# Block-sorted attention and a gated MLP: a new order of units, with whole K copies, an earlier range check and one batch's q turned by DMA

## The chip, the cores and the metric

The kernel runs on one core of a Trainium2 chip. The metric is the device time of one launch in microseconds, as the median of several runs. A core has five engines, each with its own queue of instructions that it works through in order: TensorE (PE, the matrix products; its weight loads are shown as PEld), VectorE (DVE), ScalarE (ACT), GpSimd (POOL) and SyncE (SP). Sixteen DMA engines move data between the memories. In this kernel POOL issues the loads from the chip's main memory and SP issues all other transfers.

## The reference

Each batch of attention first makes an 8x8 mixing matrix P per head by five rounds of exponential, row and column scaling. P mixes the eight blocks of k and of v. Attention runs inside each of the eight blocks. Its output is the input of a gated MLP, whose second half is normalised by row, mixed along the sequence by w_spatial, and multiplied with the first half before the last product.

```python
# attention per batch b and head h (B=4, H=8, S=768, D=64, 8 blocks of 96 rows)
P = sort_net
for _ in range(5):
    P = P - np.max(P, axis=-1, keepdims=True)
    P = np.exp(P)
    P = P / (np.sum(P, axis=-1, keepdims=True) + 1e-09)
    P = P / (np.sum(P, axis=-2, keepdims=True) + 1e-09)
...
k_sorted = np.einsum('bhij,bhjcd->bhicd', P, k_b).reshape(B, H, S, D)
v_sorted = np.einsum('bhij,bhjcd->bhicd', P, v_b).reshape(B, H, S, D)
...
scores = scale * np.matmul(q_b, k_sb.transpose(0, 1, 2, 4, 3))
scores = scores - np.max(scores, axis=-1, keepdims=True)
attn = np.exp(scores)
attn = attn / (np.sum(attn, axis=-1, keepdims=True) + 1e-09)
return np.matmul(attn, v_sb).reshape(B, H, S, D).astype(np.float32)
...
# gated MLP on x = the attention's output as (B, S, 512)
h = np.maximum(x @ w_in, 0.0)                     # w_in 512 x 1024
u, v = (h[..., :d_ff // 2].copy(), h[..., d_ff // 2:].copy())
mu = np.mean(v, axis=-1, keepdims=True)
var = np.mean((v - mu) ** 2, axis=-1, keepdims=True)
v_n = (v - mu) / np.sqrt(var + 1e-06)
v_s = np.einsum('ts,bsd->btd', w_spatial, v_n) + b_spatial[None, :, None]
gated = u * v_s
return (gated @ w_out).astype(np.float32)         # w_out 512 x 512
```

## The kernel before

The kernel is a list of short units, written as one string, ORDER (lines 18 to 48). A loop at line 692 reads it from left to right and calls the function u_NAME with the arguments behind the colons. Each unit appends its instructions to the queues of the engines that it uses, so the string fixes the order of work on every engine, on SP and on POOL's loads too; engines wait for one another through semaphores that the framework sets by tiles. Nothing is reordered afterwards.

The units, with their lines, are these. The number just behind the name is mostly one of four PSUM tiles ps0 to ps3 (two banks each); a letter is the engine of a copy (A is ACT, D is DVE, P is POOL); b is the batch, 0 to 3, and hp one of four pairs of heads.

- S0 loads sort_net. CO, ID, MA, MB, MC and IV fill constants. SK:n (L223) is round n of the scaling, alternating ACT and DVE.
- L (L156) issues a load on POOL: q, k and v of a batch (a tile of 768 KB in bf16 from a pool of eight, "ld"), both halves of w_in (wv for the normalised half, wu for the other), both halves of w_spatial (wsa, wsb), and w_out (wo).
- DM (L216) is a run of products on zeros, which nobody reads.
- PR and P0, PC, PD (L246 to L279) spread P into the matrices pd, by batch. P0 is on DVE for batch 0, PC copies P to SBUF, PD builds the later batches' pd on POOL from that copy. There are two pd tiles.
- QT and QQ (L311, L317) turn q on PE: 12 transposes for each pair of heads, then a copy out of PSUM. QT does one pair, QQ two.
- QP and QX (L337, L348) are another way to turn q, and the old order doesn't use them: QP copies a pair of heads on POOL or DVE into an ld tile in another order, and QX turns the pairs in one transposing DMA issued by SP.
- KT and VT (L370, L373) are 12 products that mix and turn k or v, with a copy by natural (L292). Its letters name the engines of the copy: with two letters, as in KT:2:DA:0:1, the first engine copies the first half of the columns and the second the rest.
- VM and VC: VM (L386) is v mixed in its natural layout, VC (L400) moves it by SP into vb, the operand of attention, one transfer for each of the blocks named.
- SC (L414) is the scores of a pair of heads and four blocks, and the exponential on ACT. AT (L459) is the product with v, the reciprocal of the sums and the scaling on DVE.
- XT and XD (L491, L482) turn the attention's output, on PE or by a transposing DMA.
- WT (L501) turns w_spatial. VP (L507) is x times the v half of w_in, for one or two row tiles of 128; ST, LN and LA (L525 to L547) are its statistics and normalisation. UP (L549) is the u half.
- SP (L564) is the mixing by w_spatial and the addition of the bias (BI loads it) into z on DVE. GT (L581) is u times z on DVE or POOL.
- OP (L588) is the last product, in some places cut into terms 0 to 3 and 3 to 4. OE (L602) copies it out of PSUM, in halves at the end, into one of two o tiles, and OS (L608) stores it by SP.
- CK (L617) tests that the attention's sums and the scaling's first sums lie in a safe range: ten small DVE instructions. CF (L632) adds up the findings with a product and leaves an integer flag. LF (L638) reads this flag into a register of every engine. At line 696 every engine branches on it: where the flag isn't zero, general_path computes everything again in a slower and safer way. BH (L641) marks a branch hint on PE and DVE.

The K copy that the change touches, and the flag read:

```python
for n, e in enumerate(eng):
    x = slice(n * 128 // len(eng), (n + 1) * 128 // len(eng))
    copy(e, to[:, x], of[:, x])
...
st["beyond"] = nc.values_load(flag[0:1, 0:1], min_val=0, max_val=512)
...
with tc.If(st["beyond"] > 0, preferred_fallthrough_block=True, label="general"):
    general_path()
```

Of the kernel before, what the change touches and what calls it, by code (L numbers as in the profile page):

```python
# [15 lines left out]


ORDER = """
S0 CO SK:0 L:q:0:0:8 L:k:0:0:8 L:v:0:0:8 L:v:1:0:8 BH SK:1 SK:2 L:k:1:0:8 ID IV:2 MC IV:0 DM:1:6:512 L:q:1:0:8 SK:3
L:wv MA DM:3:6:512 DM:1:6:512 DM:2:6:512 SK:4 L:wsb QT:1:A:0:0 MB QT:0:D:0:1 QT:3:A:0:2 DM:2:6:512 PR:3 DM:2:6:512  # L20
P0:0:2 KT:1:A:0:0 P0:6:8 L:wu P0:4:6 PC:D P0:2:4 PD:1:0:4 QT:0:D:0:3 L:wsa IV:1 PD:1:4:8 KT:2:DA:0:1 KT:3:DA:0:3
SC:1:0:0:0 SC:0:0:1:1 KT:2:D:0:2 SC:3:0:0:1 L:q:2:0:8 VT:1:D:0:0 SC:0:0:2:0 L:k:2:0:8 VT:2:D:0:1 SC:3:0:3:1 VB:1:D:0:0
VT:0:A:0:2 VB:2:D:0:1 VT:3:A:0:3 AT:1:0:0:1 VB:0:A:0:2 L:v:2:0:8 AT:2:0:0:0 L:wo VB:3:D:0:3 PD:3:0:4 SC:1:0:3:0
AT:0:0:1:1 SC:2:0:1:0 SC:3:0:2:1 AT:1:0:3:1 VM:2:A:1:0 AT:0:0:1:0 VM:3:A:1:1 AT:1:0:2:1 VM:2:A:1:2 XT:0:D:0:1:0
KT:3:A:1:2 AT:1:0:2:0 KT:0:A:1:0 AT:2:0:3:0 XT:3:A:0:1:2 KT:0:A:1:3 QQ:1:D:1:0 VM:2:A:1:3 XT:0:D:0:0:2 XT:3:D:0:0:0
SC:1:1:0:0 QQ:2:D:1:2 VC:1:0:4 KT:0:A:1:1 VP:1:D:0:0:1 SC:3:1:2:1 ST:0:0 SC:0:1:3:1 VP:2:A:0:4:5 WT:3:A:5 WT:1:D:4
VP:0:A:0:3 ST:0:5 PD:2:0:4 SC:2:1:1:0 ST:0:3 SC:1:1:2:0 UP:3:A:0:1:0 VP:2:A:0:2 VC:1:4:8 ST:0:1 ST:0:4 AT:0:1:0:0
ST:0:2 WT:1:A:3 SC:3:1:3:0 LN:0:0:6 UP:2:A:0:0:1 AT:0:1:2:0 AT:1:1:3:0 LA:0:0 PD:2:4:8 UP:3:A:0:1:1 WT:0:D:0 LA:0:2
LA:0:1 LA:0:4 AT:2:1:2:1 LA:0:3 XT:1:A:1:0:2 LA:0:5 L:v:3:0:8 WT:3:A:1 UP:0:A:0:0:0 WT:3:D:2 BI SC:1:1:0:1 QQ:2:A:2:2
AT:3:1:1:0 AT:0:1:3:1 SP:1:0:3 SC:2:1:1:1 XT:0:D:1:1:2 XT:3:A:1:0:0 AT:1:1:0:1 AT:2:1:1:1 SP:0:0:2 XT:2:A:1:1:0  # L30
GT:P:0:3 KT:1:AD:2:3 KT:3:AD:2:2 KT:0:DA:2:0 KT:2:A:2:1 GT:P:0:2 QQ:1:A:2:0 SC:0:2:3:0 VM:3:D:2:3 SP:2:0:1 VM:1:A:2:2
VM:0:A:2:1 VP:3:D:1:0:1 VM:2:A:2:0 SP:1:0:0 SC:0:2:2:1 SC:2:2:1:1 GT:P:0:1 VC:2:4:8 VC:2:0:4 ST:1:1 VP:3:A:1:4:5
SC:1:2:1:0 SC:0:2:3:1 GT:P:0:0 UP:2:A:1:0:0 PD:3:4:8 ST:1:0 ST:1:4 VP:3:D:1:2:3 VM:2:A:3:3 VM:1:A:3:0 OP:0:0:2 ST:1:2
OE:A:0:2 L:k:3:0:8 AT:1:2:3:1 VM:2:A:3:2 UP:3:A:1:1:0 ST:1:5 AT:0:2:2:1 ST:1:3 VM:2:D:3:1 L:q:3:0:8 UP:1:A:1:0:1
AT:3:2:1:1 LN:1:0:6 UP:0:A:1:1:1 LA:1:1 AT:1:2:3:0 OP:2:0:0 LA:1:0 SC:1:2:0:1 SC:0:2:2:0 OP:3:0:4 LA:1:5 OS:0:2
OE:D:0:0 LA:1:3 LA:1:4 LA:1:2 AT:2:2:0:1 AT:0:2:2:0 SP:1:1:0 OE:A:0:4 XD:2:1 SC:2:2:0:0 KT:0:DA:3:2 QQ:3:D:3:2
KT:1:D:3:1 KT:2:AD:3:0 SP:0:1:2 KT:2:A:3:3 OS:0:4 GT:D:1:0 QQ:1:A:3:0 AT:3:2:1:0 AT:0:2:0:0 VP:2:D:2:4:5 VC:3:0:4
VC:3:4:8 SC:3:3:3:0 SC:1:3:3:1 ST:2:4 XD:2:0 SP:0:1:1 SC:2:3:2:1 GT:D:1:2 SC:1:3:1:1 SP:3:1:3 AT:0:3:3:0 GT:P:1:3
AT:2:3:3:1 VP:1:A:2:2:3 ST:2:5 VP:0:A:2:0:1 OS:0:0 AT:1:3:2:1 GT:P:1:1 ST:2:3 UP:2:D:2:0:1 OP:1:1:2 SC:3:3:0:0
OE:D:1:2 ST:2:2 SC:2:3:1:0 UP:0:A:2:1:0 SC:1:3:0:1 ST:2:1 ST:2:0 LN:2:0:6 SC:3:3:2:0 UP:2:D:2:0:0 AT:0:3:1:1 LA:2:5  # L40
LA:2:4 LA:2:2 OS:1:2 UP:1:A:2:1:1 OP:2:1:0 AT:1:3:0:0 OE:A:1:0 LA:2:0 LA:2:3 LA:2:1 OP:3:1:4 AT:2:3:1:0 AT:0:3:2:0
SP:1:2:1 XD:3:0 AT:2:3:0:1 XD:3:1 GT:D:2:1 OE:A:1:4 SP:0:2:0 SP:1:2:3 GT:D:2:0 SP:0:2:2 OS:1:4 UP:3:D:3:0:0 OS:1:0
VP:0:D:3:2:3 GT:D:2:2 VP:1:A:3:0:1 ST:3:3 GT:D:2:3 ST:3:2 UP:3:A:3:0:1 VP:0:A:3:4:5 ST:3:1 OP:3:2:2 ST:3:0 OP:2:2:0
ST:3:5 ST:3:4 OE:A:2:2 LN:3:0:6 UP:1:A:3:1:1 LA:3:1 UP:0:A:3:1:0 LA:3:5 LA:3:3 LA:3:0 LA:3:2 OE:A:2:0 LA:3:4 SP:1:3:2
SP:3:3:0 GT:P:3:2 SP:0:3:1 OP:2:2:4 GT:D:3:1 OS:2:0 OS:2:2 OE:A:2:4 GT:D:3:0 SP:3:3:3 OP:1:3:0:0:3 GT:D:3:3
OP:0:3:4:0:3 OP:-1:3:0:3:4 OE:A:3:0:1:2 OP:3:3:2:0:3 CK OS:2:4 OP:-1:3:2:3:4 OE:D:3:2:1:2 OE:A:3:0:0:1 OP:-1:3:4:3:4
OS:3:0:1:2 OS:3:0:0:1 OE:A:3:2:0:1 OS:3:2:0:1 OS:3:2:1:2 OE:A:3:4:0:1 OS:3:4:0:1 OE:A:3:4:1:2 OS:3:4:1:2 CF:2 LF
"""


# [677 lines left out]
```

## Time and profile before

| what | value |
|---|---|
| median of 3 runs | 164.26 us (164.16 to 164.29) |
| the profiled execution | 163.99 us, its span 162.2 us |
| DVE, ACT, POOL busy | 117.7, 84.3, 33.7 us |
| TensorE's granted clock, mean | 0.988 |
| read from main memory, written to it | 24.78 MB, 6.29 MB |
| q copies on ACT and DVE (two pairs, L107 and L109) | 1447 and 957 ns each |
| K copies, whole, on ACT and DVE | 800 and 952 ns each |
| K copies, half, on ACT and DVE | 482 and 549 ns each |
| gate product on POOL and on DVE (L585) | 1640 and 948 ns each |
| transposing DMA (L486), issue to landing | 4.6 to 5.5 us |

The span runs from the first to the last instruction in the trace, and the profiled time is a little longer than it. Times in a trace are counted from the start of the span. The chain that ended last is found by going back from the last instruction to whatever released it, again and again, so a stretch of PE in it means that PE was the engine that everything waited for. The busy time of an engine that is not on the chain can fill up or empty without any effect on the time.

### The profile page before, as it was taken

How to read it: one execution, taken by the hardware profiler on the slowest of the kernel's cores; microseconds unless marked ns; L12 is line 12 of the kernel's file. 1: busy time of each engine (PE TensorE's matmuls, PEld its weight loads, DVE VectorE, ACT ScalarE, POOL GpSimd, SP SyncE). 2: the span in 40 equal slices, each digit the busy share in tenths (PEclk: the TensorE clock that was granted, in tenths of full speed). 3: DMA queues.
4: the chain of work that ended last, by engine and by line, in shares of the span. 5: the costliest groups of instructions: out<-in, count | busy, mean ns of one | idle time of the engine just before them, and what ended most of it. 6: DMA issues, size and time to landing. Idle time of an engine off the chain costs nothing.

```text
span 162.2 us, 3967 instructions
## 1 busy us (share of the span) xinstructions
PE 147.9 (91%) x1646; PEld 89.5 (55%) x1657; DVE 117.7 (73%) x265; ACT 84.3 (52%) x118; POOL 33.7 (21%) x39
## 2 busy tenths in 40 slices
...
DMA  2999999999999990479985996002059200243370
GB/s 12 191 204 205 203 205 205 210 220 237 271 206 204 206 172 0 69 133 148 184 188 94 225 149 195 0 36 97 0 107 237 113 0 0 91 172 129 129 250 25
DMA packets 27351, 23.20 MB, mean 143 GB/s; under 512 B 7232, under 2 KB 24128, under 8 KB 27328
## 3 DMA queue, kind: packets, MB, share of 16 engines
...
q14 instruction: 9, 0.07, 0.1%
HBM read 24.78 MB, written 6.29 MB: 192 GB/s over the span
## 4 chain that ended last, share of the span: by engine, by line
PE 78%; ACT 7%; DVE 6%; DMA 2%; issue 2%; DVEq 0%; ACTq 0%
PE ps L569 20%; PE ps L557 13%; PE ps L514 13%; PE ps L595 11%; PE ps L468 4%; PE ps L422 4%; PE ps L363 3%; PE ps L390 3%; PE ps L307 3%; ACT ex L427 2%; ACT kt L107 2%; PE ps L498 2%; DMA out_dram<-o_sb 1%; PE ps L504 1%; ACT o_sb L107 1%
## 5 line engine op out<-in xcount | busy, mean ns | idle before, releaser
L569 PE MATMUL ps<-wspT,v_sb 128*128 128x384 bf16 x192 | 33.2, 326 | 0.0
L427 ACT ACTIVATE ex<-ps 96x768 bf16<-96x768 f32 x32 | 24.4, 806 | 12.4 <-PE ps L422 12.3
L585 POOL TENSOR_TENSOR gt<-z,u_sb 128x768 bf16<-128x768 f32 x7 | 11.4, 1640 | 92.7 <-DVE z L575 42.1
L569 PEld LDWEIGHTS <-v_sb 128*128 128x128 bf16 x192 | 18.2, 98 | 11.9 <-issue 0.2
L575 DVE TENSOR_TENSOR z<-ps,b_bc 128x768 f32<-128x768 f32 x16 | 15.3, 957 | 11.6 <-PE ps L569 11.5
L557 PE MATMUL ps<-xT,w_in_sb 128*128 128x384 bf16 x128 | 23.3, 326 | 0.0
L476 DVE TENSOR_TENSOR x_sb<-ps,rec_all 96x512 bf16<-96x512 f32 x32 | 22.0, 687 | 1.1
L514 PE MATMUL ps<-w_in_sb,xT 128*128 128x512 bf16 x89 | 22.2, 379 | 0.4
L595 PE MATMUL ps<-w_out_sb,gt 128*128 128x512 bf16 x93 | 22.0, 379 | 0.2
L107 ACT COPY o_sb<-ps 128x1024 f32<-128x1024 f32 (+1 forms) x12 | 9.8, 835 | 14.8 <-PE ps L595 12.9
L531 DVE BATCH_NORM_STATS2 stats<-v_sb 128x6 f32<-128x512 bf16 x24 | 16.2, 677 | 1.0 <-ACT v_sb L113 0.9
L113 ACT ACTIVATE v_sb<-ps 128x1024 bf16<-128x1024 f32 (+1 forms) x8 | 7.4, 920 | 17.6 <-PE ps L514 17.6
L557 PEld LDWEIGHTS <-w_in_sb 128*128 128x128 bf16 x128 | 11.8, 98 | 7.6
L595 PEld LDWEIGHTS <-gt 128*128 128x128 bf16 x96 | 9.2, 98 | 10.2
L514 PEld LDWEIGHTS <-xT 128*128 128x128 bf16 x96 | 9.0, 98 | 9.6 <-DVE x_sb L476 0.2
L113 ACT ACTIVATE u_sb<-ps 128x768 bf16<-128x768 f32 x13 | 10.6, 812 | 5.1 <-PE ps L557 5.0
L107 ACT CAST kt<-ps 128x768 bf16<-128x768 f32 (+1 forms) x14 | 8.7, 641 | 7.9 <-PE ps L363 5.5
L468 PEld LDWEIGHTS <-ex 96*128 96x128 bf16 x256 | 10.5, 97 | 3.6 <-issue 0.3
L468 PE MATMUL ps<-vb,ex 96*128 96x65 bf16 x256 | 11.9, 193 | 0.1
L219 PE MATMUL ps<-warm 128*128 128x512 bf16 x35 | 9.9, 436 | 1.3 <-DVE warm L192 1.3
L422 PE MATMUL ps<-qT,kt 64*128 64x96 bf16 x256 | 9.5, 204 | 1.6 <-ACT kt L107 1.3
L422 PEld LDWEIGHTS <-kt 64*128 64x128 bf16 x256 | 6.2, 94 | 6.9 <-issue 3.8
...
## 6 DMA issues: line engine op xcount, KB each, us to landing
...
```

Of the source, the lines that this page charges most:

```text
L107: nc.scalar.copy(out=out, in_=in_)
L113: nc.scalar.activation(out=out, in_=in_, func=AF.Relu)
L422: nc.tensor.matmul(t[:, hh, 0:HW].rearrange("p (g x) -> p g x", g=G)[:, :, ii * TB:(ii + 1) * TB], lhsT=kT[rows, i * BLK:i * BLK + 128], r ...
L427: nc.scalar.activation(out=e_tile(b, hp, ih).rearrange("p h (x g) -> p h x g", g=G), in_=t[0:BLK, :, 0:HW].rearrange("p h (g x) -> p h x g ...
L468: nc.tensor.matmul(t[:, hh, ii * VW:ii * VW + D + 1], lhsT=e[:, c:c + 128], rhs=vb[b % 2][:, ih * NI + ii, 2 * hp + hh, 0:D + 1], start=Tr ...
L476: nc.vector.tensor_mul(out=x_sb[:, hp].rearrange("p i (h d) -> p h i d", h=2), in0=tv[:, :, :, 0:D], in1=_raw_ap(rec, 0, [rec.ap[0], [NI, ...
L514: nc.tensor.matmul(t[:, x, :], lhsT=st["xT", b][:, n // 3, kc, (n % 3) * 128:(n % 3 + 1) * 128], rhs=w_in_sb[:, kc, DH:DFF], start=(kc == ...
L531: nc.vector.bn_stats(out=stats, in_=st["v_sb", b, n])
L557: nc.tensor.matmul(t[:, x, 0:HW], lhsT=w_in_sb[:, kc, mc * 128:(mc + 1) * 128], rhs=st["xT", b][:, ih, kc, :], start=(kc == 0), stop=(kc = ...
L569: nc.tensor.matmul(t[:, x, 0:HW], lhsT=st["v_sb", b, n][:, mc * 128:(mc + 1) * 128], rhs=wspT[:, 3 * x:3 * x + 3, n, :], start=(n == 0), s ...
L575: nc.vector.tensor_add(out=z.rearrange("p (x c) -> p x c", x=2), in0=t[:, :, 0:HW], in1=b_bc.rearrange("p (x c) -> p x c", x=2),)
L595: nc.tensor.matmul(t[:, x, :], lhsT=st["gt", b, mc][:, (n0 + x) * 128:(n0 + x + 1) * 128], rhs=w_out_sb[:, mc, :], start=(mc == 0), stop=( ...
```

## The change

Only the string ORDER differs, and the functions are the same ones. All units that compute something occur in both, apart from these differences:

- Seven KT units had two letters, so that two engines each copied a half. Now each KT has one letter; ten are on ACT and six on DVE.
- The two QQ units of batch 3 are gone. In their place four QP units on POOL follow the load of q of batch 3, which now stands ahead of v's and k's of that batch, and one QX unit stands on SP between the two halves of VC for batch 2.
- CK, CF and LF stood at the very end. CK now follows the last AT unit, CF follows soon after, and LF stands ahead of the last VP unit.
- BH moves from the start into the second batch's attention.
- The order of nearly all other units is new, with other PSUM tiles and, for some copies and gate products, other engines. The four VM units of batch 1 stand earlier, the pd of batch 3 is built ahead of that of batch 2, and the loads have a new order too.

```diff
--- before.py
+++ after.py
@@ -16,35 +16,36 @@
 
 
 ORDER = """
-S0 CO SK:0 L:q:0:0:8 L:k:0:0:8 L:v:0:0:8 L:v:1:0:8 BH SK:1 SK:2 L:k:1:0:8 ID IV:2 MC IV:0 DM:1:6:512 L:q:1:0:8 SK:3
-L:wv MA DM:3:6:512 DM:1:6:512 DM:2:6:512 SK:4 L:wsb QT:1:A:0:0 MB QT:0:D:0:1 QT:3:A:0:2 DM:2:6:512 PR:3 DM:2:6:512
-P0:0:2 KT:1:A:0:0 P0:6:8 L:wu P0:4:6 PC:D P0:2:4 PD:1:0:4 QT:0:D:0:3 L:wsa IV:1 PD:1:4:8 KT:2:DA:0:1 KT:3:DA:0:3
-SC:1:0:0:0 SC:0:0:1:1 KT:2:D:0:2 SC:3:0:0:1 L:q:2:0:8 VT:1:D:0:0 SC:0:0:2:0 L:k:2:0:8 VT:2:D:0:1 SC:3:0:3:1 VB:1:D:0:0
-VT:0:A:0:2 VB:2:D:0:1 VT:3:A:0:3 AT:1:0:0:1 VB:0:A:0:2 L:v:2:0:8 AT:2:0:0:0 L:wo VB:3:D:0:3 PD:3:0:4 SC:1:0:3:0
-AT:0:0:1:1 SC:2:0:1:0 SC:3:0:2:1 AT:1:0:3:1 VM:2:A:1:0 AT:0:0:1:0 VM:3:A:1:1 AT:1:0:2:1 VM:2:A:1:2 XT:0:D:0:1:0
-KT:3:A:1:2 AT:1:0:2:0 KT:0:A:1:0 AT:2:0:3:0 XT:3:A:0:1:2 KT:0:A:1:3 QQ:1:D:1:0 VM:2:A:1:3 XT:0:D:0:0:2 XT:3:D:0:0:0
-SC:1:1:0:0 QQ:2:D:1:2 VC:1:0:4 KT:0:A:1:1 VP:1:D:0:0:1 SC:3:1:2:1 ST:0:0 SC:0:1:3:1 VP:2:A:0:4:5 WT:3:A:5 WT:1:D:4
-VP:0:A:0:3 ST:0:5 PD:2:0:4 SC:2:1:1:0 ST:0:3 SC:1:1:2:0 UP:3:A:0:1:0 VP:2:A:0:2 VC:1:4:8 ST:0:1 ST:0:4 AT:0:1:0:0
-ST:0:2 WT:1:A:3 SC:3:1:3:0 LN:0:0:6 UP:2:A:0:0:1 AT:0:1:2:0 AT:1:1:3:0 LA:0:0 PD:2:4:8 UP:3:A:0:1:1 WT:0:D:0 LA:0:2
-LA:0:1 LA:0:4 AT:2:1:2:1 LA:0:3 XT:1:A:1:0:2 LA:0:5 L:v:3:0:8 WT:3:A:1 UP:0:A:0:0:0 WT:3:D:2 BI SC:1:1:0:1 QQ:2:A:2:2
-AT:3:1:1:0 AT:0:1:3:1 SP:1:0:3 SC:2:1:1:1 XT:0:D:1:1:2 XT:3:A:1:0:0 AT:1:1:0:1 AT:2:1:1:1 SP:0:0:2 XT:2:A:1:1:0
-GT:P:0:3 KT:1:AD:2:3 KT:3:AD:2:2 KT:0:DA:2:0 KT:2:A:2:1 GT:P:0:2 QQ:1:A:2:0 SC:0:2:3:0 VM:3:D:2:3 SP:2:0:1 VM:1:A:2:2
-VM:0:A:2:1 VP:3:D:1:0:1 VM:2:A:2:0 SP:1:0:0 SC:0:2:2:1 SC:2:2:1:1 GT:P:0:1 VC:2:4:8 VC:2:0:4 ST:1:1 VP:3:A:1:4:5
-SC:1:2:1:0 SC:0:2:3:1 GT:P:0:0 UP:2:A:1:0:0 PD:3:4:8 ST:1:0 ST:1:4 VP:3:D:1:2:3 VM:2:A:3:3 VM:1:A:3:0 OP:0:0:2 ST:1:2
-OE:A:0:2 L:k:3:0:8 AT:1:2:3:1 VM:2:A:3:2 UP:3:A:1:1:0 ST:1:5 AT:0:2:2:1 ST:1:3 VM:2:D:3:1 L:q:3:0:8 UP:1:A:1:0:1
-AT:3:2:1:1 LN:1:0:6 UP:0:A:1:1:1 LA:1:1 AT:1:2:3:0 OP:2:0:0 LA:1:0 SC:1:2:0:1 SC:0:2:2:0 OP:3:0:4 LA:1:5 OS:0:2
-OE:D:0:0 LA:1:3 LA:1:4 LA:1:2 AT:2:2:0:1 AT:0:2:2:0 SP:1:1:0 OE:A:0:4 XD:2:1 SC:2:2:0:0 KT:0:DA:3:2 QQ:3:D:3:2
-KT:1:D:3:1 KT:2:AD:3:0 SP:0:1:2 KT:2:A:3:3 OS:0:4 GT:D:1:0 QQ:1:A:3:0 AT:3:2:1:0 AT:0:2:0:0 VP:2:D:2:4:5 VC:3:0:4
-VC:3:4:8 SC:3:3:3:0 SC:1:3:3:1 ST:2:4 XD:2:0 SP:0:1:1 SC:2:3:2:1 GT:D:1:2 SC:1:3:1:1 SP:3:1:3 AT:0:3:3:0 GT:P:1:3
-AT:2:3:3:1 VP:1:A:2:2:3 ST:2:5 VP:0:A:2:0:1 OS:0:0 AT:1:3:2:1 GT:P:1:1 ST:2:3 UP:2:D:2:0:1 OP:1:1:2 SC:3:3:0:0
-OE:D:1:2 ST:2:2 SC:2:3:1:0 UP:0:A:2:1:0 SC:1:3:0:1 ST:2:1 ST:2:0 LN:2:0:6 SC:3:3:2:0 UP:2:D:2:0:0 AT:0:3:1:1 LA:2:5
-LA:2:4 LA:2:2 OS:1:2 UP:1:A:2:1:1 OP:2:1:0 AT:1:3:0:0 OE:A:1:0 LA:2:0 LA:2:3 LA:2:1 OP:3:1:4 AT:2:3:1:0 AT:0:3:2:0
-SP:1:2:1 XD:3:0 AT:2:3:0:1 XD:3:1 GT:D:2:1 OE:A:1:4 SP:0:2:0 SP:1:2:3 GT:D:2:0 SP:0:2:2 OS:1:4 UP:3:D:3:0:0 OS:1:0
-VP:0:D:3:2:3 GT:D:2:2 VP:1:A:3:0:1 ST:3:3 GT:D:2:3 ST:3:2 UP:3:A:3:0:1 VP:0:A:3:4:5 ST:3:1 OP:3:2:2 ST:3:0 OP:2:2:0
-ST:3:5 ST:3:4 OE:A:2:2 LN:3:0:6 UP:1:A:3:1:1 LA:3:1 UP:0:A:3:1:0 LA:3:5 LA:3:3 LA:3:0 LA:3:2 OE:A:2:0 LA:3:4 SP:1:3:2
-SP:3:3:0 GT:P:3:2 SP:0:3:1 OP:2:2:4 GT:D:3:1 OS:2:0 OS:2:2 OE:A:2:4 GT:D:3:0 SP:3:3:3 OP:1:3:0:0:3 GT:D:3:3
-OP:0:3:4:0:3 OP:-1:3:0:3:4 OE:A:3:0:1:2 OP:3:3:2:0:3 CK OS:2:4 OP:-1:3:2:3:4 OE:D:3:2:1:2 OE:A:3:0:0:1 OP:-1:3:4:3:4
-OS:3:0:1:2 OS:3:0:0:1 OE:A:3:2:0:1 OS:3:2:0:1 OS:3:2:1:2 OE:A:3:4:0:1 OS:3:4:0:1 OE:A:3:4:1:2 OS:3:4:1:2 CF:2 LF
+S0 L:q:0:0:8 CO L:k:0:0:8 ID L:v:0:0:8 SK:0 SK:1 L:v:1:0:8 L:k:1:0:8 SK:2 IV:2 SK:3 L:q:1:0:8 IV:0 MA SK:4 DM:0:6:512
+DM:2:6:512 MC MB IV:1 L:wv L:wu L:wsb DM:3:6:512 L:wsa DM:2:6:512 QT:1:A:0:0 QT:0:D:0:3 QT:2:A:0:2 DM:3:6:512
+QT:1:A:0:1 PR:2 P0:0:2 L:q:2:0:8 DM:3:6:512 PC:A KT:1:A:0:0 P0:2:4 P0:6:8 P0:4:6 KT:2:D:0:1 KT:3:D:0:2 SC:1:0:0:1
+KT:0:D:0:3 SC:2:0:1:0 VT:1:A:0:0 VT:3:D:0:1 SC:2:0:1:1 SC:0:0:2:0 PD:1:4:8 VB:1:D:0:0 SC:3:0:0:0 PD:1:0:4 VB:2:D:0:1
+VT:0:A:0:2 AT:1:0:0:1 SC:3:0:3:0 AT:2:0:1:0 VB:0:D:0:2 L:v:2:0:8 SC:1:0:2:1 VM:3:D:1:3 VM:2:A:1:0 VM:1:A:1:2
+AT:0:0:0:0 VM:3:A:1:1 AT:2:0:2:1 L:wo VT:1:A:0:3 AT:0:0:1:1 SC:3:0:3:1 PD:3:4:8 KT:2:A:1:1 VB:1:D:0:3 KT:0:A:1:3
+XT:3:D:0:1:0 XT:2:A:0:0:0 L:k:2:0:8 AT:1:0:3:1 KT:0:A:1:0 AT:3:0:2:0 KT:2:A:1:2 AT:1:0:3:0 QQ:0:A:1:2 XT:2:D:0:1:2
+QQ:3:D:1:0 PD:3:0:4 XT:2:A:0:0:2 VP:1:D:0:4:5 SC:2:1:3:1 ST:0:5 VC:1:4:8 ST:0:4 SC:0:1:0:1 VP:3:A:0:0:1 AT:2:1:0:1
+VP:0:A:0:3 PD:2:0:4 ST:0:1 VP:1:A:0:2 SC:3:1:3:0 SC:2:1:2:1 VC:1:0:4 ST:0:3 UP:0:A:0:1:1 WT:1:A:5 ST:0:2 ST:0:0
+LN:0:0:6 AT:3:1:3:1 UP:2:D:0:1:0 AT:0:1:2:1 SC:1:1:0:0 BH UP:3:A:0:0:0 LA:0:4 AT:2:1:3:0 LA:0:3 LA:0:5 PD:2:4:8
+L:q:3:0:8 UP:0:A:0:0:1 LA:0:0 WT:3:D:4 SC:1:1:2:0 LA:0:2 SC:2:1:1:1 WT:0:D:3 WT:3:A:1 LA:0:1 QQ:1:D:2:2 QP:P:3:2
+QP:P:3:0 SC:0:1:1:0 AT:2:1:0:0 BI QP:P:3:3 WT:3:A:0 WT:1:D:2 XT:0:A:1:1:2 AT:2:1:1:0 AT:3:1:2:0 SP:1:0:3 QP:P:3:1
+VM:0:A:2:0 GT:D:0:3 QQ:2:A:2:0 AT:3:1:1:1 VM:1:D:2:1 SP:0:0:2 VM:2:A:2:3 XT:3:A:1:1:0 GT:D:0:2 SP:1:0:0 VM:3:A:2:2
+VC:2:4:8 QX:3:0:4 XT:2:D:1:0:2 VP:0:D:1:4:5 XT:2:A:1:0:0 SP:3:0:1 ST:1:4 VC:2:0:4 KT:2:A:2:1 KT:0:A:2:2 KT:1:A:2:3
+KT:3:D:2:0 VP:2:D:1:2:3 ST:1:3 SC:1:2:0:1 SC:3:2:2:1 VP:0:D:1:0:1 L:v:3:0:8 GT:P:0:1 GT:P:0:0 ST:1:5 SC:2:2:3:1 ST:1:0
+SC:1:2:1:1 UP:3:A:1:0:0 SC:0:2:1:0 AT:1:2:3:1 OP:2:0:2 ST:1:2 OE:A:0:2 VM:3:A:3:1 AT:0:2:2:1 ST:1:1 UP:1:A:1:1:1
+AT:2:2:0:1 AT:0:2:1:1 OP:3:0:0 LN:1:0:6 LA:1:3 LA:1:1 L:k:3:0:8 LA:1:2 LA:1:4 VM:2:A:3:0 LA:1:0 VM:1:A:3:2 XD:2:1
+OE:A:0:0 OS:0:2 LA:1:5 UP:0:A:1:0:1 VM:2:A:3:3 SP:1:1:0 OS:0:0 VC:3:0:4 SC:3:2:3:0 KT:2:D:3:1 SC:0:2:2:0 KT:1:A:3:2
+KT:3:A:3:3 KT:0:D:3:0 SC:2:2:0:0 UP:1:A:1:1:0 AT:3:2:2:0 AT:2:2:1:0 SP:0:1:2 GT:P:1:2 OP:2:0:4 UP:0:A:2:1:1 OE:D:0:4
+GT:P:1:0 AT:3:2:3:0 AT:1:2:0:0 SP:2:1:1 SC:0:3:0:0 VC:3:4:8 SC:3:3:1:0 SP:1:1:3 SC:2:3:0:1 SC:0:3:2:0 OS:0:4
+VP:3:A:2:4:5 GT:P:1:1 AT:1:3:2:0 AT:2:3:0:0 XD:2:0 VP:0:A:2:0:1 SC:3:3:3:0 SC:1:3:3:1 VP:2:A:2:2:3 GT:P:1:3
+UP:3:A:2:1:0 ST:2:4 ST:2:1 ST:2:0 ST:2:5 AT:0:3:3:0 AT:1:3:3:1 ST:2:2 OP:2:1:0 OE:A:1:0 AT:3:3:1:0 AT:0:3:0:1
+UP:1:A:2:0:0 ST:2:3 OP:2:1:2 LN:2:0:6 LA:2:5 LA:2:2 LA:2:0 LA:2:4 SC:0:3:2:1 OE:A:1:2 SC:3:3:1:1 LA:2:3 UP:1:D:2:0:1
+LA:2:1 OP:0:1:4 AT:2:3:1:1 AT:3:3:2:1 SP:1:2:2 CK OS:1:0 XD:3:0 OE:A:1:4 GT:D:2:2 UP:0:D:3:0:0 VP:1:A:3:0:1 SP:2:2:0
+CF:0 ST:3:0 OS:1:4 GT:P:2:0 SP:3:2:3 SP:0:2:1 GT:P:2:3 ST:3:1 XD:3:1 VP:2:A:3:2:3 ST:3:3 LF VP:3:A:3:4:5 ST:3:2 ST:3:5
+UP:2:A:3:1:1 ST:3:4 GT:P:2:1 OP:0:2:0 LN:3:0:6 OS:1:2 OE:A:2:0 OP:3:2:4 LA:3:4 LA:3:0 LA:3:2 LA:3:1 UP:0:A:3:1:0
+LA:3:3 LA:3:5 UP:1:A:3:0:1 SP:0:3:1 SP:1:3:0 GT:D:3:0 GT:D:3:1 SP:0:3:2 OE:A:2:4 OP:2:2:2 GT:D:3:2 SP:1:3:3 OS:2:0
+OP:3:3:0:0:3 OP:1:3:2:0:3 OS:2:4 GT:D:3:3 OP:-1:3:0:3:4 OE:A:2:2 OP:0:3:4:0:3 OS:2:2 OE:A:3:0:0:1 OP:-1:3:2:3:4
+OE:D:3:2:1:2 OE:A:3:0:1:2 OS:3:0:0:1 OS:3:0:1:2 OE:D:3:2:0:1 OP:-1:3:4:3:4 OS:3:2:1:2 OE:D:3:4:1:2 OE:A:3:4:0:1
+OS:3:2:0:1 OS:3:4:0:1 OS:3:4:1:2
 """
```

## The prediction

> **What bounds the kernel.** I read the totals first, then the chain that ended last, then TensorE's gaps on it, DMA by slice, and the tail.
>
> ```profile
> span 162.2 us, 3967 instructions
> PE 147.9 (91%) x1646; PEld 89.5 (55%) x1657; DVE 117.7 (73%) x265; ACT 84.3 (52%) x118; POOL 33.7 (21%) x39
> ...
> DMA  2999999999999990479985996002059200243370
> ...
> PE 78%; ACT 7%; DVE 6%; DMA 2%; issue 2%; DVEq 0%; ACTq 0%
> ```
>
> TensorE (PE) is the chain for 78% of the span. The DMA row shows loads back to back until 61 us: each q, k or v batch lands about 3.85 us after the one before (q0 8.75, k0 12.58, v0 16.41), later q1 28.74, the v half of w_in 31.28, q2 47.13, the fifteenth load 61.20. The first product with w_in (VP of batch 0) starts at 32.83; from there the chain by time is nearly all PE. The largest hole:
>
> ```profile
> 55.97 0.80 ACT xT L107
> 56.76 0.39 ACT kt L107
> ...
> 57.18 0.42 DVE kt L109
> ...
> 58.12 0.56 DVE kt L109
> ...
> 58.70 0.49 ACT kt L107
> ...
> 59.23 0.34 PE ps L422 x8
> ```
>
> Here the halves of a split K copy run one after the other on two engines, not side by side. The tail:
>
> ```profile
> L639 PEldq TENSOR_LOAD <-flag x1: 490/490/490, 153.6 to 153.6; - x1
> L639 ACTq TENSOR_LOAD <-flag x1: 477/477/477, 154.4 to 154.4; - x1
> L639 SPq TENSOR_LOAD <-flag x1: 912/912/912, 156.2 to 156.2; - x1
> ...
> L696 SPq EVENT_SEMAPHORE  x8: 17/17/17, 157.7 to 160.0; - x8
> ```
>
> The flag read delays SP from 156.2 to 157.7, but SP then waits until 159.8 for the last store to land; the closing barrier takes 2.2 us more.
>
> **The parts.** Lengths per unit on the chain when PE runs back to back: SP 1.95 us (12 products), UP 1.30, VP 0.87 a row tile, OP 0.216 a product, QQ 0.67, KT and WT 0.34, XT 0.40, VM 0.33, AT 0.24, SC 0.22. From the first VP on, the old order has 116.0 us of these and takes 152.9 - 32.8 = 120.1; 0.9 of the difference is idle at the split copies (0.29 before the q transposes, 0.58 before SC), about 3.2 are small handovers that I carry over unchanged.
>
> *K copies.* Seven split copies (halves 0.48 on ACT, 0.55 on DVE, in sequence 1.03) become whole ones at 0.80 or 0.95. Early ones cost nothing, since q1 and w_in land later. At 56 to 59 us the gap of 0.87 goes: after the four KT of batch 2 now stand a VP of 1.73 us, which covers the last copy. Without that cover a copy of 0.95 would show. **-0.9** (0 to -1.4).
>
> *q of batch 3.* Two QQ leave PE (-1.34); ACT loses a copy of 1.45 and DVE one of 0.96. Counted from the first VP, an SC more now stands behind it, so 114.9 remain against 116.0: **-1.1**. Added are four QP copies on POOL (128x768 bf16), an ld tile and one transposing DMA. QP has no row. Below: 768 elements at POOL's one-input slope (affine select of 128 in 0.295 against about 0.11 for one element, 1.45 ns each) give 1.2 us, less at the memset slope (1.1 ns, 0.95). Above: its two-input product of 768, 1.64. I take 1.2, the row with one input; four are 4.8 (3.8 to 6.6).
> In the Trainium skill, GPSIMD Engine Reference, section 3.1, one input costs 1.03 cycles an element and two about 2.6 at 1.2 GHz; the two-input row (1.64 us for 768, 2.1 ns) agrees. By it a QP would be an estimated 0.7 us, the four 2.0 us less than in my sum.
>
> The DMA (24 blocks of 128 rows) is costed from XD (16 of 96 rows: issue 1.46, landing 5.1, some 3 of it moving). Issue 2.2 to 2.9, landing 5.1 to 10, taken 8. It sits on SP between the two halves of VC:2; behind it wait the second half, then XD:2:1 and the stores.
>
> *What POOL holds up.* POOL now waits in the QP for q3, the fifteenth load, about 61.2. Then 4.8 of QP to 66.0, then L:v:3 (0.9), then two gate products (1.64 each) to 70.2, then L:k:3. A load's first packets come 1.2 after its issue (batch-3 k here: issued by 71.4, moving at 72.6) and it moves for 3.85 alone, up to 7.7 if the transpose takes half; I take 5.8. So v3 lands at 66.0+0.9+1.2+5.8 = 73.9 (71 to 77.5). PE wants it at VM:3:A:3:1, 39.1 us of units behind the first VP. On the same stretch the old order (36.9 of units to the same kind of place) ran to 72.55, 1.9 over its units and the gap; 32.6+39.1+1.9 = 73.6. **+0.3** (0 to +3). The others are covered: the gate products at 70.2 stand against their OP at 71.9; k3 some 4 behind v3 against its KT at 82.1; the DMA done by 76 against its first SC at 93; VC:2's second half about 75 against its first AT at 85.
>
> *Start of the products.* The VM of batch 1 stand earlier, and their copies, by a walk along ACT and DVE, end near 25, not 31.2. So the eight VC:1 transfers and the bias load start about 6 us earlier, among q1 and w_in. In the old run, q2 took 5.80 after the load before it, where these ran, against 3.85. If the whole 3.2 us that the loads lost there fell ahead of w_in, the first VP would be 2.1 later than now; with none of it, at 31.3. I take 32.6: **-0.2** (-1.5 to +2.1).
>
> *Range check and flag.* CK's ten DVE instructions (about 2 us) stand behind the last AT; CF and the flag come 12 and 6 us of PE units after that, so nobody waits for them. The read itself (LF) stands in every engine's queue before the last VP: 0.49 on PE, 0.54 on DVE, 0.48 on ACT, 0.49 on POOL, 0.91 plus 0.3 on SP. PE is the path: 0 if products in flight cover it, 0.6 with restart; I take **+0.5**, since nothing in its row shows PE running on. Behind it on SP stand only stores; ACT and DVE have 50 and 40% idle there. At the tail its removal is worth nothing: the last landing hides it. There the last tile's copy is now split over DVE and ACT, one after the other (0.69+0.59 against 1.07, +0.2), while the stores of the tile before leave some 0.4 earlier: **-0.1** (-1 to +0.5).
>
> *New order, VectorE.* DVE's units (AT 0.87, ST 0.82, SP's add 0.96 and so on) over the first 25 us of PE units behind VP are 24.4 us, formerly 22.8 over 26.6. At 97% some PSUM tile comes free late. **+0.5** (0 to +2.5).
>
> **Sum**: -0.9-1.1+0.3-0.2+0.5-0.1+0.5 = -1.0. The profiled execution took 163.99 (span 162.2 and 1.8 around it), so 163.0 for one like it; the median of runs is 164.26, 0.27 more, and the same step from there gives **163.3**.
>
> **Rivals.** *No new wait shows* (the read, v3 and DVE cost nothing): -2.3, 162.0. For it: PE's units alone; against: three queues fuller at once.
> *POOL's queue ends it, slower.* q3, four copies, then the load of v: with copies at 1.64 and the transpose beside the load, v3 lands at 61.2+6.6+0.9+1.2+6.3 = 76.2 against 73.6. Price 2.6 instead of 0.3, +1.3, 165.6; it decides from a landing after 74.9, where the whole gain is gone. For it: POOL has no other work to put ahead; against: the one-input rows.
> The Trainium skill, DMA: Bandwidth & Descriptors, section on queues, rings and completion order, has each DMA engine take turns between its queues packet by packet; the 5.80 against 3.85 agrees, and by that rule the load beside the transpose would move for nearer 7.7.
> *DVE becomes the bound* in the 25 us behind VP: +2.5, with v3's wait swallowed, +0.7, 165.0. For it the 97%, against it that the old order had 142% in one stretch of 6 us without a visible gap.
> *w_in late*: first VP at 34.9, v3's wait swallowed, +1.0, 165.3. For it 25 against 31 us, against it that a VC packet needed 5 us to get through the backlog.
> *Whole copies gain nothing*, since the gap was PSUM turnover: 164.2, inside the forecast's own spread.
>
> **Chances.** Forecast 0.42 (own range 162.5 to 164.3), no new wait 0.17, POOL 0.20, DVE 0.12, w_in 0.09. A difference of 0.2% (163.93 to 164.59) is about what can be told here. Faster: 0.34 of the forecast and 0.17, 0.51. Same: 0.08 of the forecast, 0.02 of w_in, 0.10. Slower: 0.20+0.12+0.07 = 0.39. The range reaches from below 162.0, for a better tail, to above 165.6, for v3 at 77: 161.3 to 166.0.
>
> **What would show it.** Right: no idle before L422 and L307 after batch 2's KT; QP rows near 1.2; idle of PE at L390 for v_in under 1; a PE hole of 0.5 at L639 with nothing waiting for the flag; first L514 near 32.6; SP's last waits still ended by a landing. Wrong: a hole of over 2 at L390 behind v_in, PE waits on x_sb or z copies between 40 and 58, a first L514 after 34, or QX landing after its SC asks for q.

## The result and the profile after

The changed kernel takes 171.31 us (170.88 to 172.66, four runs), the kernel before 164.27 us (164.16 to 164.50) on the same chip: a ratio of 1.044 with an interval of 1.0376 to 1.0505. It is slower by 7.0 us, outside the predicted range of 161.3 to 166.0. Where a ratio below compares fewer runs than the times beside it, runs over 1.5% above the fastest of their kernel are left out of it (one of e2, two of e8, whose profile is one of these).

All code behind ORDER has moved down by one line, so L595 before is L596 after. From the page of the profiled execution (170.89 us), the span, the busy times, three rows of the 40 slices (PE, its granted clock, the DMA engines) and the chain's shares:

```profile
span 169.1 us, 3863 instructions
...
PE 150.8 (89%) x1597; PEld 89.0 (53%) x1609; DVE 113.3 (67%) x256; ACT 84.3 (50%) x116; POOL 40.0 (24%) x45
...
PE   6999999999999999990099999999999999999920
...
PEclk9999999999999999997559999999999999999985
DMA  2999999999999968999902743400917120330363
...
PE 55%; issue 18%; DMA 7%; POOL 6%; DVE 5%; SPq 3%; ACT 2%; DVEq 0%; ACTq 0%; POOLq 0%
```

TensorE has two empty slices, 4.2 us each, and the granted clock falls to a half in the second of them and in the one behind. Before, the two rows had no such hole:

```profile
PE   6988999899999979999999999999999999999700
...
PEclk9999999999999999999999999999999999999995
```

PE's share of the chain is 55% (78% before), since the chain now runs through POOL, SP and a DMA for part of its length; most of the 18% of "issue" is the 27.1 us in which POOL stands ahead of the QP copies until q of batch 3 has landed. The list of PE's waits has only one entry that matters:

```profile
engine line waited for: us in total, times, longest us
PE ps L596 <- ACT vm L108: 7.8, 1, 7.8
```

Columns are the line that waited, what it waited for, the sum, the count and the longest. Line 596 is OP, line 108 a copy by ACT, and vm the tile that holds v in its natural layout. The chain that ended last passes through the same place (start, length, what), and shows what the copy itself waited for:

```profile
61.18 3.12 POOL qp L344 x4
64.30 0.74 POOL v_in L163
...
68.40 2.67 SPq L351
...
71.13 1.21 SPq L404
...
73.71 9.30 DMA vb<-vm
...
83.31 0.81 ACT vm L108
...
84.16 3.57 PE ps L596 x8
87.72 1.14 PE ps L391 x4
```

Read it from below. OP waits for a PSUM tile that the VM copy on ACT reads out. That copy writes vm, and waits until a transfer that reads vm (VC of batch 2, line 404) has landed at 83.01. That transfer was issued only at 73.71, because SP was held by QX (line 351) until 71.08. The timeline (start, length, engine, line, in brackets the idle time before and its end) gives the lengths:

```profile
64.33 6.75 SPq L351 DMA_TRANSPOSE qT<-qp  x1
...
71.13 3.17 SPq L404 DMA_DIRECT2D vb<-vm  x4
...
83.31 0.80 ACT L108 CAST vm<-ps 128x768 bf16<-128x768 f32 x1 [8.38 <-DMA vb<-vm]
...
84.16 3.57 PE L596 MATMUL ps<-w_out_sb,gt 128*128 128x512 bf16 x8 [7.78 <-ACT vm L108]
```

ACT stood ready at 74.93 (83.31 less 8.38). Why the transfers took so long is told by the issue and the last landing of each, worked out from the trace's semaphore events:

```
                              issued   last landing
v of batch 3 (POOL)            64.25      73.80
QX, all of batch 3's q (SP)    64.33      81.55
k of batch 3 (POOL)            68.34      81.34
VC:2, second half, 1st (SP)    71.13      81.92
VC:2, second half, 4th (SP)    73.71      83.01
```

QX and the two loads share the DMA engines until 81.5, and the four small transfers, issued on SP behind QX, land one after the other right behind it.

The windows show the clock (PE busy and count, other engines, then granted clock, DMA share and GB/s):

```profile
72.00:76.00 4.00, 3.95 (x40) 2.18 (x37) 3.41 (x9) 2.08 (x3) 0.00 (x0) 1.00 1.37 172
76.00:80.00 4.00, 0.37 (x13) 0.28 (x10) 1.91 (x6) 0.00 (x0) 0.00 (x0) 0.79 1.47 155
80.00:84.00 4.00, 0.00 (x0) 0.00 (x0) 0.00 (x0) 0.69 (x1) 0.00 (x0) 0.50 1.10 254
84.00:88.00 4.00, 3.85 (x10) 1.43 (x10) 2.03 (x6) 1.21 (x4) 0.00 (x0) 0.50 0.23 91
88.00:92.00 4.00, 4.00 (x25) 2.30 (x23) 0.00 (x0) 3.60 (x5) 0.00 (x0) 0.93 0.06 24
```

PE goes idle at 76.4, the clock is halved from 78.36 to 88.60 (its records in the trace), and so the first 4.4 us of work behind the hole run at half speed: eight OP products take 3.57 us against 1.73 (eight at 0.216), four of VM 1.14 against 0.65. The hole thus costs 7.78 + 1.84 + 0.49 = 10.1 us.

The account of the whole, by profiled executions (the end of the last product is the start of the last group of L595 or L596 and its 5.34 us):

| us | before | after | difference |
|---|---|---|---|
| first product with w_in | 32.83 | 32.36 | -0.5 |
| from there to the end of the last product | 120.1 | 129.2 | +9.0: the hole 10.1, all else -1.1 |
| from there to the end of the span | 9.2 | 7.6 | -1.7 |
| span | 162.2 | 169.1 | +6.9 |

So without the hole this execution would have been some 3 us faster than before. (The differences are taken before rounding.)

### The profile page after: what moved, and what is told of

It is laid out like the page before. It is cut to its first block, busy times and chain, and to the rows that moved or that the text cites. A ratio compares the mean times of both kernels' runs of the same rounds, so it can differ in the third digit from the quotient of the medians.

```text
span 169.1 us, 3863 instructions
## 1 busy us (share of the span) xinstructions
PE 150.8 (89%) x1597; PEld 89.0 (53%) x1609; DVE 113.3 (67%) x256; ACT 84.3 (50%) x116; POOL 40.0 (24%) x45
## 4 chain that ended last, share of the span: by engine, by line
PE 55%; issue 18%; DMA 7%; POOL 6%; DVE 5%; SPq 3%; ACT 2%; DVEq 0%; ACTq 0%; POOLq 0%
PE ps L570 14%; PE ps L596 11%; PE ps L558 8%; PE ps L515 6%; DMA vb<-vm 6%; PE ps L220 5%; PE ps L469 3%; PE ps L364 3%; POOL pd L276 2%; POOL qp L344 2%; PE ps L423 2%; DVE kt L110 2%; SPq L351 2%; SPq L404 1%; DMA out_dram<-o_sb 1%
## 5 line engine op out<-in xcount | busy, mean ns | idle before, releaser
L596 PE MATMUL ps<-w_out_sb,gt 128*128 128x512 bf16 x92 | 23.5, 400 | 8.0 <-ACT vm L108 7.8
L586 POOL TENSOR_TENSOR gt<-z,u_sb 128x768 bf16<-128x768 f32 x9 | 14.7, 1641 | 57.9 <-DVE z L576 34.7
L596 PEld LDWEIGHTS <-gt 128*128 128x128 bf16 x96 | 9.5, 101 | 18.8 <-issue 9.6
L108 ACT CAST vm<-ps 128x768 bf16<-128x768 f32 x10 | 7.7, 808 | 16.4 <-DMA vb<-vm 8.4
L114 ACT ACTIVATE v_sb<-ps 128x1024 bf16<-128x1024 f32 (+1 forms) x9 | 8.4, 929 | 14.3 <-PE ps L515 14.2
L544 DVE TENSOR_SCALAR v_sb<-v_sb,mv,rstd 128x512 bf16<-128x512 bf16 x24 | 8.4, 406 | 8.5 <-ACT rstd L539 8.5
L220 PE MATMUL ps<-warm 128*128 128x512 bf16 x35 | 10.7, 470 | 1.4 <-DVE warm L193 1.3
L469 PEld LDWEIGHTS <-ex 96*128 96x128 bf16 x256 | 10.1, 97 | 3.0 <-ACT ex L428 0.2
L344 POOL COPY qp<-q_in 128x768 bf16<-128x768 bf16 x4 | 3.1, 820 | 27.2 <-DMA q_in<-in_q_dram 27.2
```

The lines of the kernel that those rows point to most:

```text
L108: nc.scalar.copy(out=out, in_=in_)
L114: nc.scalar.activation(out=out, in_=in_, func=AF.Relu)
L220: nc.tensor.matmul(t[:, 0, 0:int(w)], lhsT=warm[:, 0:128], rhs=warm[:, 0:int(w)], start=True, stop=True)
L469: nc.tensor.matmul(t[:, hh, ii * VW:ii * VW + D + 1], lhsT=e[:, c:c + 128], rhs=vb[b % 2][:, ih * NI + ii, 2 * hp + hh, 0:D + 1], start=Tr ...
L596: nc.tensor.matmul(t[:, x, :], lhsT=st["gt", b, mc][:, (n0 + x) * 128:(n0 + x + 1) * 128], rhs=w_out_sb[:, mc, :], start=(mc == 0), stop=( ...
```

## The experiments

The theory: the second half of VC:2, late behind QX, holds up the VM copies of batch 3, because both use the one tile vm. Rivals: the traffic of QX itself (its landing, or what it does to the loads) is the cost wherever it stands; the half clock is a large part by itself; other parts of the change lose as well.

**e1: the second half issued ahead of QX.**

```diff
-VC:2:4:8 QX:3:0:4 XT:2:D:1:0:2 ... ST:1:4 VC:2:0:4
+VC:2:4:8 VC:2:0:4 QX:3:0:4 XT:2:D:1:0:2 ... ST:1:4
```

> The changed kernel with one unit moved: the second half of VC for batch 2 is issued by SP ahead of the transposing DMA QX, not behind it. Theory 1 (place in SP's queue: vm is one tile, the ACT copy of batch 3's first VM waits until that half has been read out of it, and it sat behind QX): the PE idle of 7.8 us at 76.4 to 84.2 and the half clock after it (products that took 3.57 us for 1.73, and some more, 2.3 us together) go, 170.9 - 10.1 = 160.8, from 160 to 162. Theory 2 (the transposing DMA beside the loads is itself the cost, wherever it stands): PE still loses 4 us or more near there, 165 or above.

Measured: 163.44 us (162.69 to 165.0), ratio 0.9973 (0.9933 to 1.0013). One moved unit returns 7.9 us, and PE's wait for vm is gone. But it is 2.6 us above the forecast for it, and above the range. The queue of SP in its timeline:

```profile
60.54 5.72 SPq L404 DMA_DIRECT2D vb<-vm  x8
66.36 11.67 SPq L351 DMA_TRANSPOSE qT<-qp  x1
78.22 5.88 SPq L487 DMA_TRANSPOSE xT<-x_sb  x1
```

QX now holds SP for 11.67 us and lands at 84.87, 18.5 after its issue. Beside it k of batch 3 lands at 83.81, and PE waits 1.1 us for it. The rival of the traffic has a part in it; e6 tries that part.

**e2: two vm tiles, by batch.** The order is the one of the changed kernel. To find the room, v_sb and gt have five buffers instead of six, and the warm-up products (DM) are 384 wide, eight for six.

```diff
-    vm = const.tile([128, G, H, VW], BF16, name="vm")
+    vms = [const.tile([128, G, H, VW], BF16, name=f"vm{n}") for n in range(2)]
...
-            vm[:, :, 2 * hp:2 * hp + 2, 0:D].rearrange("p g h d -> p h g d"),
+            vms[b % 2][:, :, 2 * hp:2 * hp + 2, 0:D].rearrange("p g h d -> p h g d"),
```

> The changed kernel in its own order, with two vm tiles used in turn by batch, so that batch 3's VM writes where the late transfers do not read (room for it: v_sb and gt have five buffers instead of six, and the warm tile is 384 wide with 8 dummy products for 6). Theory 1: the ACT copy no longer waits though the second half still lands near 83, so 160.8 to 162.5, up to 1 us more than with the second half first because the first product with vb's first four blocks may have to wait for that landing. Theory 2 or a late load of v of batch 3: the idle stays at 4 us or more, 166 to 171.

Measured: 161.71 us (161.34 to 161.77 where compared), ratio 0.9854 (0.9835 to 0.9874). QX still holds SP for 8.54 us and the second half still lands between 80.45 and 83.08, as late as before; PE's longest wait behind 62 us is 0.5, for k:

```profile
PE ps L364 <- DMA k_in<-in_k_dram: 0.5, 1, 0.5
```

The late transfer alone costs nothing: it is the reuse of vm that turns it into a hole. That wait is worth 171.3 - 161.7 = 9.6 us, close to the 10.1 from the trace.

**e3: q of batch 3 on PE again**, in the new order.

```diff
-... QP:P:3:2 QP:P:3:0 ... QP:P:3:3 ... QP:P:3:1 ... QX:3:0:4 ...
-SC:2:2:0:0 UP:1:A:1:1:0 ... SP:0:1:2 GT:P:1:2
+SC:2:2:0:0 QQ:3:D:3:0 UP:1:A:1:1:0 ... SP:0:1:2 QQ:1:A:3:2 GT:P:1:2
```

> The changed kernel with QP and QX taken out and the two QQ units of batch 3 put back on PE among batch 3's KT and scores. Theory 1: with QX gone the second half of VC is on time, so no idle at 76 to 84; PE has 1.34 us more: 160.8 + 1.3 = 162.1, 161 to 163. If turning q by DMA saved nothing at all, this equals the run with the second half first.

Measured: 163.27 us (163.19 to 163.48), ratio 0.9954 (0.9937 to 0.9970), a little above the expected range. With QX away the hole is gone too, and the rest of the change is worth -0.8. As long as the second half only stands ahead of QX (e1, 163.44), turning q by DMA brings nothing.

**e4: only the whole K copies**, in the kernel before: all seven KT units with two letters get one.

```diff
-KT:2:DA:0:1 KT:3:DA:0:3 ... KT:1:AD:2:3 KT:3:AD:2:2 KT:0:DA:2:0 ... KT:0:DA:3:2 ... KT:2:AD:3:0
+KT:2:D:0:1 KT:3:A:0:3 ... KT:1:A:2:3 KT:3:D:2:2 KT:0:D:2:0 ... KT:0:A:3:2 ... KT:2:D:3:0
```

> The kernel before with one part of the change alone: its seven split K copies made whole, on one engine each. The prediction's step: the 0.9 us of PE idle at 56 to 59 goes, 164.27 - 0.9 = 163.4. Rival (the gap was the turnover of PSUM tiles, not the split): 164.2.

Measured: 163.49 us (163.09 to 163.78), ratio 0.9965 (0.9953 to 0.9976), so -0.6. PE still waits up to 0.6 us at SC for a K copy: in the old order no VP stands behind the four KT of batch 2.

**e5: the hole filled with products**, so that the clock stays up: after AT:0:2:1:1 in the changed kernel.

```diff
-AT:0:2:1:1 OP:3:0:0
+AT:0:2:1:1 DM:2:31:512 OP:3:0:0
```

> The changed kernel with 31 dummy products (6.7 us) put where PE stands idle, ahead of the first product of the last-but-two output that waits; the wait itself stays. Theory 1a (of the 9.6 us that the wait on vm costs, some 2 are the half clock that PE was granted after standing idle): the clock stays at 1.0, the eight products after the gap take 1.73 us again, and the time falls by about 2: 171.3 - 2 = 169.3, from 168.5 to 170. Rival (the idle alone costs it all and the clock is hidden): no change, 171.

Measured: 171.14 us (170.09 to 171.99), ratio 1.0397 (1.0368 to 1.0427). The windows, as above:

```profile
76.00:80.00 4.00, 3.14 (x25) 1.51 (x22) 1.90 (x6) 0.00 (x0) 0.00 (x0) 1.00 1.58 169
80.00:84.00 4.00, 4.00 (x19) 1.75 (x18) 0.00 (x0) 0.00 (x0) 0.00 (x0) 1.00 1.00 158
84.00:88.00 4.00, 2.35 (x13) 1.12 (x12) 1.14 (x4) 1.92 (x5) 0.00 (x0) 1.00 0.73 217
```

The clock stays at 1.00. In this execution QX held SP for 8.61 us and the second half landed at 84.59, so OP started at 85.74, 1.58 later than in the changed kernel, yet the last product ended at 160.94 against 161.54. From the start of that OP to the end of the last product it needed 75.2 us, as e6 does, which has no hole; the changed kernel needed 77.4. The full clock is therefore worth about 1.58 + 0.6 = 2.2 us here. It doesn't show in the time, which is the one that the rival had forecast: in this execution the transfers came later and the stretch behind the last product took 9.3 us against 7.6. So the clock's part is read from this one trace, the one of the longest of the four runs. By it the half clock is a consequence of the hole and a fifth of its price, not a cause.

**e6: the loads first as well.** As e1, and v and k of batch 3 are loaded right behind q, ahead of the QP copies in POOL's queue.

```diff
-L:q:3:0:8 UP:0:A:0:0:1
+L:q:3:0:8 L:v:3:0:8 L:k:3:0:8 UP:0:A:0:0:1
...
-VP:0:D:1:0:1 L:v:3:0:8 GT:P:0:1
+VP:0:D:1:0:1 GT:P:0:1
...
-LA:1:1 L:k:3:0:8 LA:1:2
+LA:1:1 LA:1:2
```

> The kernel with the second half of VC first, and on POOL the loads of v and k of batch 3 issued ahead of the four QP copies, not behind them. Theory 3 (what was left over against the two-vm kernel is traffic: the transposing DMA held SP for 11.7 us beside the two loads and k landed at 83.8, 1.1 us after PE asked): both loads land by about 69, the transpose is issued in under 5 us and lands by 76, no wait of PE on v or k of batch 3: 163.4 - 1.1 - 0.5 = 161.8, from 161.0 to 162.3. Rival (the transpose is as slow by itself): its issue stays over 8 us and the time at 163.

Measured: 161.75 us (161.61 to 161.91), ratio 0.9848 (0.9832 to 0.9864). v lands at 65.42 and k at 71.95. SP's queue:

```profile
60.47 5.30 SPq L404 DMA_DIRECT2D vb<-vm  x8
65.88 6.72 SPq L351 DMA_TRANSPOSE qT<-qp  x1
77.88 1.42 SPq L487 DMA_TRANSPOSE xT<-x_sb  x1
```

QX lands 8.8 us after its issue instead of 18.5, and PE's waits for v and k are gone. The time is as expected, the issue is not: it still takes 6.72 us. Against e3, which has the loads in their old places, q by DMA together with the earlier loads is now worth -1.5.

**e7: only the range check and the read moved**, in the kernel before.

```diff
-XD:3:1 GT:D:2:1 ... UP:3:D:3:0:0 OS:1:0 ... ST:3:2 UP:3:A:3:0:1
+XD:3:1 CK GT:D:2:1 ... UP:3:D:3:0:0 CF:1 OS:1:0 ... ST:3:2 LF UP:3:A:3:0:1
...
-OP:3:3:2:0:3 CK OS:2:4 ... OS:3:4:1:2 CF:2 LF
+OP:3:3:2:0:3 OS:2:4 ... OS:3:4:1:2
```

> The kernel before with one part of the change alone: CK after its last AT, CF after the first UP of batch 3, LF ahead of the last but one UP of that batch's first half. The prediction's step: +0.5 for the read on PE and nothing at the tail, 164.1 + 0.5 = 164.6. After the changed kernel's trace (the read took 0.49 us on PE and products ran on without a hole): 0.0 from the read, so 164.1, from 163.7 to 164.3.

Measured: 164.71 us (164.59 to 165.11), ratio 1.0030 (1.0019 to 1.0041), +0.4, above the range expected after the trace. Its largest wait of PE behind the start:

```profile
PE ps L569 <- DVE z L575: 1.3, 1, 1.3
```

An SP unit waits for DVE's addition of the bias, behind CK's ten instructions, which DVE works through from 120.37 to 122.19. The read is no part of this wait: it comes on PE at 128.7, and no PE wait is listed there. The early place of the check is followed up in e10.

**e8: the loads first, but the second half left behind QX**: e6 without e1's edit.

> The changed kernel with only the loads of v and k of batch 3 put ahead of the QP copies; the second half of VC stays behind the transposing DMA. Theory 1 with 3 (the place costs what the transpose takes, and beside no loads that is 4 to 5 us of issue and a landing by 76): the second half lands near 77 instead of 83, PE idles some 2 us instead of 7.8 and keeps its clock: 163 to 165. Theory 1 alone (the place costs 9.6 us whatever else moves): 170 or more.

Measured: 163.92 us (162.03 to 165.03), ratio 0.9897 (0.9863 to 0.9931) from the two runs at 162.03 and 163.11. In the profiled execution, the one at 165.03, QX lands at 73.42 and the second half at 77.33:

```profile
PE ps L596 <- ACT vm L108: 2.3, 1, 2.3
...
78.47 3.56 PE L596 MATMUL ps<-w_out_sb,gt 128*128 128x512 bf16 x8 [2.25 <-ACT vm L108]
```

With the loads out of the way, the same place behind QX costs 2.3 us of waiting instead of 7.8. The clock was expected to hold, but it is halved from 78.52 to 81.93, and from this OP to the end of the last product PE needs 76.9 us against 75.2 in e6, so the short hole costs 1.7 us more. The two shorter runs are 0.3 and 1.4 us above e6; how long PE waited in them is not known. So the hole is a product of two things, the place of the second half and the traffic around QX.

**e9: QX with no load beside it.** As e6, but QX stands later, when all loads have landed.

```diff
-VC:2:0:4 QX:3:0:4 XT:2:D:1:0:2
+VC:2:0:4 XT:2:D:1:0:2
...
-XD:2:1 OE:A:0:0
+XD:2:1 QX:3:0:4 OE:A:0:0
```

> The kernel with the second half of VC first and both loads ahead of the copies, and the transposing DMA of q put behind the first transposing DMA of batch 2's output (XD), where no load of POOL is under way. Theory 4 (what stretched its issue from some 3 us to 6.7, 8.6 and 11.7 is the loads and VC transfers beside it): issued in 2.2 to 3.5 us, landed within 8 of its start, about 88, in time for its first scores near 91 to 93; time as in the run with the loads first, 161.8, from 161.4 to 162.6. Rival (24 blocks of 128 rows are slow by themselves, not in proportion to XD's 1.46 us for 16 blocks of 96): an issue of over 5 us again, and the transfers behind it (VC of batch 3) late.

Measured: 161.67 us (161.55 to 162.19), ratio 0.9852 (0.9829 to 0.9874), as e6. SP's queue:

```profile
77.90 1.56 SPq L487 DMA_TRANSPOSE xT<-x_sb  x1
79.56 4.28 SPq L351 DMA_TRANSPOSE qT<-qp  x1
```

Without loads, QX holds SP for 4.28 us and lands 6.2 after its issue. It is not quite alone: the XD ahead of it lands only at 82.11. Neither forecast had that length: of the 6.75 at most 4.3 go with the transfer itself, and the rest with the traffic.

**e10: the check and the read at the end**, in e6.

```diff
-SP:1:2:2 CK OS:1:0 ... SP:2:2:0 CF:0 ST:3:0 ... ST:3:3 LF VP:3:A:3:4:5
+SP:1:2:2 OS:1:0 ... SP:2:2:0 ST:3:0 ... ST:3:3 VP:3:A:3:4:5
...
-GT:D:3:3 OP:-1:3:0:3:4 ... OS:3:4:1:2
+GT:D:3:3 CK OP:-1:3:0:3:4 ... OS:3:4:1:2 CF:2 LF
```

> The kernel with the second half of VC first and both loads ahead of the copies, and CK, CF and LF put back at the end, as in the kernel before. If the check amid the last batch costs in this order too (alone in the old order it cost 0.44 us, through CK's 2 us on DVE ahead of a z that PE waited for): 161.75 - 0.4 = 161.3. If this order covers CK: 161.8, no difference; if the read at the end is not hidden by the last landing here, 0.3 to 0.8 slower, 162.3.

Measured: 162.78 us (162.61 to 163.07), ratio 0.9914 (0.9898 to 0.9930), so in this order the early check is worth -1.0, more than any of the forecasts had. PE's last product ends 0.3 us earlier than in e6 (150.93 against 151.27), so the cost lies behind it. The answer on the store's line for the last two stores (durations of the issue in ns, then landing in us), in e10:

```profile
L611 SPq DMA_DIRECT2D out_dram<-o_sb x2: 333/355/377, 153.8 to 154.3; - x2
...
DMA to landing us min/median/max: 2.9/3.6/4.2
```

and the same in e6:

```profile
L611 SPq DMA_DIRECT2D out_dram<-o_sb x2: 332/358/383, 154.5 to 154.9; - x2
...
DMA to landing us min/median/max: 2.4/2.4/2.5
```

Both stores leave 0.7 us earlier, yet the last of them lands 1.0 later (158.44 against 157.49). In the kernel before, the last three took 4.0 to 4.2 us as well. With the read last, one 16 KB packet of the instruction queues, 1.06 us long, runs on a DMA engine at 155.7 while the stores move, and three of 8 KB just before it; in e6 there are two of 8 KB alone (154.67 and 155.23). That these packets delay the landing was not tried by itself.

## Why the prediction was wrong

**The step that failed** is the one in the costing of q of batch 3: "It sits on SP between the two halves of VC:2; behind it wait the second half, then XD:2:1 and the stores", with the cover "VC:2's second half about 75 against its first AT at 85". Two things in it were wrong, and it took both.
- The landing: 83.0, not 75. I let QX hold SP for 2.2 to 2.9 us and land 8 after its issue, from XD, which moves less and mostly alone; it held SP for 6.75 and landed after 17.2.
- The waiter: I named the reader of the transfer's target (AT at 85) and not the next writer of its source. vm is one tile, and batch 3's VM copies write it; ACT was ready for the first at 74.93.

With the landing at 75 the missing waiter would have cost nothing, and with AT as the only waiter a landing at 83 costs nothing, which is e2 (161.7). Put together they are a hole of 7.8 us, and 10.1 with the clock.

The Trainium skill, DMA: Bandwidth & Descriptors, section on queues, rings and completion order, says that each DMA engine goes round its queues packet by packet. The prediction used this for the load of v only. The runs agree with it in the other direction too: the transpose lands 6.2 us after its issue with no load beside it (e9), 8.8 beside the rest of k's load (e6), and 17.2 and 18.5 with two loads beside it (the changed kernel, e1).

The other terms:
- *K copies*, -0.9 predicted: -0.6 alone in the old order (e4), where a wait of 0.6 stays. In the changed order no PE wait for a K copy is left, as predicted. PE's timeline there has the four KT of batch 2, the VP that covers the last copy, and SC, without an idle time in brackets:

```profile
63.92 1.64 PE L364 MATMUL ps<-pd,k_in 128*64 128x128 bf16 x48
...
65.50 1.90 PE L515 MATMUL ps<-w_in_sb,xT 128*128 128x512 bf16 x7
...
67.33 0.51 PE L423 MATMUL ps<-qT,kt 64*128 64x96 bf16 x16
```

- *q of batch 3*, -1.1: -1.5 by e6 against e3, where it is placed well (the earlier loads counted in), and about 0 in e1. QP took 0.82 us, not 1.2 (the page's group, mean ns behind the comma):

```profile
L344 POOL COPY qp<-q_in 128x768 bf16<-128x768 bf16 x4 | 3.1, 820 | 27.2 <-DMA q_in<-in_q_dram 27.2
```

  The prediction's estimate of 0.7 by the figure in the Trainium skill, GPSIMD Engine Reference, section 3.1, is nearer.
- *What POOL holds up*, +0.3: v landed at 73.80 (73.9 predicted), and PE's weight load for the VM (L391) waited 0.46. This is right by two errors that cancel: the four copies were 1.7 us shorter, and the load beside QX was as much longer (9.55 from issue to landing). The rival of POOL's queue took the right pair, a transpose beside a load, but looked for the delay at the load; the transfers behind the transpose had it.
- *Start of the products*, -0.2: -0.5 (32.36) between these two executions. Over all traces it is 32.3 to 32.6 in the new order and 32.6 to 32.9 in the old, so nearer to -0.3.
- *Flag*, +0.5 on PE: nothing. The rows of the read on SP and PE in the changed kernel (duration in ns, then its start):

```profile
L640 SPq TENSOR_LOAD <-flag x1: 469/469/469, 133.1 to 133.1; - x1
...
L640 PEldq TENSOR_LOAD <-flag x1: 487/487/487, 134.1 to 134.1; - x1
```

and the window of PE around it (busy us and products, granted clock, DMA share, GB/s):

```profile
134.00:135.00 1.00, 1.00 (x8) 1.00 0.14 53
```

  PE's queue takes 0.49 us for it and its products go on without a gap.
- *Tail*, -0.1: -1.7 in the profiled execution. That "the last landing hides it" was wrong, since the landing itself is later with the read at the end: the stretch behind the last product is 9.2 to 9.9 us in the three kernels that read last (before, e4, e10), and 7.6 to 9.3 in the nine that read early. What spreads it among the nine is open.
- *New order*, +0.5 for DVE: PE has no wait for DVE of over 0.2 us behind 32 us in the changed kernel, though CK's place can cost (e7).

The terms gave -1.0, and the trace without the hole gives -3.2 (-0.5, -1.1, -1.7): flag, tail and DVE were priced too high. e2, which has no hole, is 2.4 us below the kernel before on the same chip (161.71 against 164.06), which is nearer to the rival "No new wait shows" (-2.3) than to the forecast. The list of signs didn't name the one that appeared, a wait of L596 for vm; it looked at L390 for v_in and at SC for q.

The versions e2, e6 and e9 beat both kernels: 161.71, 161.75 and 161.67 us, 1.5% below the kernel before.
